# Keys, values and queries of two token tiles as one product of seven multiplications

## The chip, the cores and the metric

The kernel runs on one core of a Trainium2 chip. Its time is the device time of one execution in microseconds (us); of several executions the median counts, and less is better.

## The reference

A block of 2048 tokens with width 576: a layer norm, linear attention with 32 heads of width 18, and a feed-forward path of width 4608 whose gated result multiplies what attention gives. All inputs are float32. Cut to what matters:

```python
phi = lambda t: jnp.where(t > 0, t + 1, jnp.exp(t)) + 1e-6
xn = layernorm(x)                                   # x: (1, 2048, 576)
q, k, v = heads(xn @ wqkv)                          # wqkv: (576, 3 * 576), 32 heads of 18
pq, pk = phi(q), phi(k)
kv = jnp.einsum("bhsd,bhse->bhde", pk, v)           # one 18 x 18 state for each head
z = jnp.einsum("bhsd->bhd", pk)
num = jnp.einsum("bhqd,bhde->bhqe", pq, kv)
den = jnp.einsum("bhqd,bhd->bhq", pq, z)[..., None] + 1e-6
s = merge_heads(num / den) @ wo                     # wo: (576, 576)
g = silu(gelu(xn @ w1 + b1) @ w2 + b2)              # w1: (576, 4608), w2: (4608, 576)
return x + s * g
```

## The kernel before

**Number format.** A float32 value is split into a high part, rounded to the format that TensorE multiplies at full speed (fp32r), and a low part, the rest. A product of two such values is three matmuls: high by high, high by low, low by high. The 576 rows of a contraction are five k-tiles: four of 128 rows, and a fifth that holds 64 rows twice, high parts above low parts, so that it needs two matmuls and not three. A token tile is 128 tokens; there are NT = 16.

**Order.** The two attention stages stand under `in_order()`: on each engine the instructions run in the order in which the program text issues them. SyncE (SP) issues nearly all DMAs, in text order too. In the feed-forward the order is written out by a planner (`add`, `at_step`), which gives each step of a chunk its place beside the matmuls.

**Stage one, keys and values (loop `for t in range(NT)`, 0 to about 145 us).** For each token tile `load_x` brings the rows for `statistics` (two `bn_stats` on VectorE, the inverse root by `pow` on GpSimd, POOL). The first four tiles are normalized on ScalarE (L227) and transposed by TensorE. For the others x comes transposed from memory; `store_stats` writes mean and inverse deviation of the 128 tokens to memory, `load_stats` reads them back as a row on all partitions (`bc`), `center` subtracts on POOL (L282), `scale` multiplies on VectorE (L285), and `set_x_hi`, `set_x_lo` split. All parts stay on chip, as `xh` and `xl`. `project` (L310 to L325, its matmul is L321) multiplies the tile with the weights `wkv_h`, `wkv_l`: keys and a first group of values in 28 matmuls (tile `pk`), the other values in 14 (`pv`). `phi` makes three ScalarE passes (L334, L336, L338) and a VectorE maximum (L340). `state` (L379) adds the keys' products with the values, of the tile before, into the banks `ps_kva` and `ps_kvb`.

Beside this stand operands for the feed-forward. `w2_load` brings the blocks of W2 for one of nine chunks into a raw tile (`w2r`, two alternate), `w2_sum` (L405, POOL) forms two differences, `w2_hi` (L413, ScalarE) and `w2_lo` (L418, VectorE) split them, and `w2_store` writes them to memory; `we_*` do the same for sums of W1's last rows, in five parts.

**Between the stages.** `fold_wo` multiplies the masked state with the output weights and gives `kw`, which `split_kw` splits.

**Stage two, queries and output (loop `for i in range(1, NT + 4)`, about 162 to 283 us).** `query` multiplies a token tile with the query weights, 28 matmuls of `project` (tile `pq`); `phi` again; `by_sums` and `normalize` form the denominators (POOL, VectorE) and p = phi(q) / den on POOL (L753); `pad` (ScalarE) copies 64 columns; `transpose_p` transposes p on TensorE (tile `ptp`) and splits it; `attend` (matmul L788) multiplies it with `kw` in 28 matmuls, and the result goes to memory (`s_dram`):

```python
    for i in range(1, NT + 4):
        if 1 < i < NT:
            query(i)
        ...
        if 2 <= i < NT + 2:
            transpose_p(i - 2)
        if 2 <= i < NT + 1:
            pad(i - 1)
        beside(i, 2)
        if i < NT:
            normalize(i)
        if i >= 4:
            attend(i - 4)
```

Beside it `XSums` forms on VectorE the sums of x that the first feed-forward product needs, `Rest` gathers the 64 remaining rows through memory (L925 to L973), and W1 and W2 operands of the first chunks are loaded and split.

**The feed-forward.** Two halves of 1024 tokens, nine chunks each, 28 steps to a chunk of some 44.7 us. The first product (class `Up`, L1129 to L1185) takes a block 2 x 2 by 2 x 2 with seven block products in place of eight (sums of blocks as operands, the 64 rest rows added in), and so does the second (`product`, L1273). At the change of halves (640.9 to 685.6 us) the x operands of the second half are loaded by `load_x_part` (L1446) in seven transfers of 1 MB.

The functions that the change touches, as they stand before it:

## Time and profile before

| | before |
|---|---|
| median of three runs | 1103.26 us |
| lowest, highest | 1101.92, 1103.40 us |
| span of the profiled execution | 1096.2 us |
| TensorE matmuls (PE) | 1088.2 us busy, 99% |
| TensorE weight loads (PEld) | 1008.8 us, 92% |
| VectorE (DVE) | 829.5 us, 76% |
| ScalarE (ACT) | 491.3 us, 45% |
| GpSimd (POOL) | 471.5 us, 43% |
| mean granted TensorE clock | 0.999 |
| transfers | 262.54 MB, mean 239 GB/s |

The profile is of one execution. Its span is from the first to the last instruction; for its own time only the timed runs stand, whose median is 7.06 us above the span, so that a number of the profile is compared with 1096.2 and the kernel's time with 1103.26. A row of costly groups has line, engine, operation, result and operands, their shapes and the count, then the busy time of all and the mean ns of one, then the engine's idle time before them with the instruction that ended most of it. A row of the chain in order of time has start, length, engine, tile and line. A row of windows has the stretch, its length, and the busy time and the instructions of PE, PEld, DVE, ACT and POOL, then the granted clock, the share of the DMA engines and GB/s; where it begins with "a:b" the first figure after it is the length.

### The profile page before, as it was taken

To read this page: it belongs to the slowest core of one execution; us is meant where nothing else is said; L and a number is where in the kernel's file an instruction comes from. 1 tells how busy PE (TensorE), PEld (TensorE's weight loads), DVE (VectorE), ACT (ScalarE), POOL (GpSimd) and SP (SyncE) were. 2 spreads that over 40 slices of the span, in tenths; PEclk is the share of its full clock that TensorE was granted. 3 is DMA by queue.
4 is the path that set the end of the run, shared out by engine and by line. 5 is a ranking of instruction groups with operands and counts; after the bars stand their busy time and mean duration, and the time that the engine had idled before them with its cause. 6 is when DMAs were issued, how large, how long until landed. Compare 5 with 4: busy or idle time off the path is not lost.

```text
span 1096.2 us, 18083 instructions
## 1 busy us (share of the span) xinstructions
PE 1088.2 (99%) x6702; PEld 1008.8 (92%) x6702; DVE 829.5 (76%) x1132; ACT 491.3 (45%) x844; POOL 471.5 (43%) x403
## 2 busy tenths in 40 slices
PE   9999999999999999999999999999999999999998
PEld 8999989999898998989989989899898998989987
DVE  7787748888798888888888888667475584764856
ACT  6555555555545455454453544524234243242442
POOL 3676434323546446464554553424234143242340
PEclk9999999999999999999999999999999999999999
DMA  7898834675959558486585769978676676767452
GB/s 248 264 274 274 309 137 149 206 248 186 333 221 350 182 220 322 160 320 224 189 332 175 284 237 400 391 248 289 215 241 219 210 231 212 238 219 224 126 184 87
DMA packets 88400, 262.54 MB, mean 239 GB/s; under 512 B 11894, under 2 KB 24182, under 8 KB 85624
## 3 DMA queue, kind: packets, MB, share of 16 engines
q1 hardware_dynamic: 88312, 261.38, 69.3%
q8 instruction: 53, 0.87, 0.3%
q14 instruction: 35, 0.29, 0.1%
HBM read 164.24 MB, written 95.17 MB: 237 GB/s over the span
## 4 chain that ended last, share of the span: by engine, by line
PE 99%; DVE 1%; ACT 0%; issue 0%; POOL 0%; DVEq 0%; POOLq 0%
PE pm L1286 35%; PE a L1147 10%; PE e L1147 10%; PE zy L1147 10%; PE pk L321 6%; PE pq L321 5%; PE ps_s L788 5%; PE b L1147 5%; PE pv L321 4%; PE pd L1402 2%; PE ps_kva L382 1%; PE ptp L770 1%; PE ps_kw L707 1%; PE warm L369 0%; DVE wkv_l L364 0%; PE ps_kvb L382 0%
## 5 line engine op out<-in xcount | busy, mean ns | idle before, releaser
L1292 DVE TENSOR_TENSOR macc<-pm,macc 128x576 f32<-128x576 f32 x218 | 163.9, 752 | 49.9 <-PE pm L1286 48.4
L812 ACT CAST h_h<-g 128x512 fp32r<-128x512 f32 x204 | 121.9, 621 | 132.7 <-PE pm L1286 131.5
L815 DVE TENSOR_TENSOR h_l<-g,h_h 128x512 fp32r<-128x512 f32 x204 | 161.8, 800 | 0.0
L1252 POOL TENSOR_TENSOR mid<-g 128x512 f32<-128x512 f32 x34 | 43.9, 1292 | 108.1 <-ACT g L1155 108.1
L1246 POOL TENSOR_TENSOR g<-g 128x512 f32<-128x512 f32 x34 | 54.9, 1616 | 49.5 <-DVE h_l L815 28.4
L1155 ACT ACTIVATE g<-b,b1c 128x512 f32<-128x512 f32 x36 | 24.8, 690 | 102.5 <-DVE b L1173 102.5
L1164 ACT COPY mid<-a 128x512 f32<-128x512 f32 x36 | 21.1, 585 | 95.3 <-PE a L1147 95.3
L858 POOL TENSOR_TENSOR w1raw<-w1raw 128x256 f32<-128x256 f32 x18 | 13.3, 737 | 116.8 <-ACT h_h L812 68.2
L1167 DVE TENSOR_TENSOR mid<-b,mid 128x512 f32<-128x512 f32 x36 | 24.8, 690 | 45.0 <-PE b L1147 41.8
L1374 POOL TENSOR_TENSOR fin1l<-fin1h,fin1l 128x288 f32<-128x288 f32 x8 | 6.5, 811 | 118.4 <-DMA fin1l<-s_dram 69.6
L1249 POOL TENSOR_TENSOR g<-g 128x512 f32<-128x512 f32 x34 | 55.2, 1623 | 2.7
L1147 PE MATMUL a<-h0r,wa 128*128 128x512 f32 x144 | 50.4, 390 | 0.0
L1147 PE MATMUL a<-xh,wa 128*128 128x512 f32 x144 | 50.4, 390 | 0.0
L815 DVE TENSOR_TENSOR h_l<-mid,h_h 128x512 fp32r<-128x512 f32 x34 | 48.8, 1436 | 1.2
L1155 ACT ACTIVATE g<-e,b1c 128x512 f32<-128x512 f32 x36 | 24.8, 690 | 51.9 <-DVE e L1180 51.9
L753 POOL TENSOR_TENSOR pbuf<-phiq,den 128x576 f32<-128x576 f32 x16 | 19.4, 1213 | 63.6 <-DVE den L752 63.6
L1243 POOL TENSOR_TENSOR g<-g 128x512 f32<-128x512 f32 x34 | 44.1, 1296 | 2.7
L1180 DVE TENSOR_TENSOR e<-e,mid 128x512 f32<-128x512 f32 x36 | 24.8, 690 | 22.3 <-PE e L1147 22.3
L1170 DVE TENSOR_TENSOR mid<-zy,mid 128x512 f32<-128x512 f32 x36 | 24.9, 691 | 19.8 <-PE zy L1147 19.8
L1173 DVE TENSOR_TENSOR b<-e,mid 128x512 f32<-128x512 f32 x36 | 25.2, 700 | 18.5 <-PE e L1147 17.4
L321 PE MATMUL pk<-wkv_h,xh 128*128 128x288 f32 (+1 forms) x160 | 38.2, 321 | 0.4 <-ACT xh L248 0.4
L321 PE MATMUL pk<-wkv_l,xh 128*128 128x288 f32 (+1 forms) x160 | 38.4, 321 | 0.0
(857 smaller groups left out, 3646.5 us busy)
## 6 DMA issues: line engine op xcount, KB each, us to landing
we<-we_dram SPq DMA_DIRECT2D x36, 448.0 KB
w2raw<-w SPq DMA_DIRECT2D x10, 1152.0 KB
op<-w2o SPq DMA_DIRECT2D x18, 576.0 KB
w1raw<-w SPq DMA_DIRECT2D x18, 512.0 KB
op_a<-wa SPq DMA_DIRECT2D x18, 512.0 KB
op_c<-wc SPq DMA_DIRECT2D x18, 512.0 KB
op_d<-wd SPq DMA_DIRECT2D x18, 512.0 KB
wc<-op_c SPq DMA_DIRECT2D x18, 512.0 KB
```

Source lines behind the costliest of these rows:

```text
L321: nc.tensor.matmul(ps[:, h, : ws.stop - ws.start], st, w[:, k, ws], start=(begin and i == 0), stop=(end and i == len(seq) - 1), skip_group ...
L788: nc.tensor.matmul(ps[:, h, :HD], st[:, k, :], w[:, k, h * HD : (h + 1) * HD], start=(i == 0), stop=(i == len(seq) - 1),)
L812: nc.scalar.copy(pair[0], src)
L815: eng.tensor_tensor(pair[1], src, pair[0].bitcast(F32), op=SUB)
L1147: nc.tensor.matmul(ps, st, mv, start=first and n == 0, stop=n == len(seq) - 1, skip_group_check=True,)
L1155: nc.scalar.activation(g, ps, AF.Gelu_apprx_tanh, bias=b1c[:, f : f + 1])
L1243: tt(src[5, pr], A(1, 0), A(1, 1), op=ADD)
L1246: tt(src[6, pr], src[5, pr], A(0, 0), op=SUB)
L1249: tt(src[3, pr], A(0, 1), src[6, pr], op=SUB)
L1252: tt(src[7, pr], A(0, 0), A(1, 0), op=SUB)
L1286: nc.tensor.matmul(ps[:, q, :HD], hs[p][st][:, cs], m[:, p, :], start=(n == 0 and i not in CHAIN), stop=(n == 5), skip_group_check=True,)
L1292: nc.vector.tensor_tensor(dst, src, dst, op=ADD)
```

## The change

The token tiles go in eight pairs. For a pair, the normalized x of its two tiles by the columns of keys, values and queries (half of keys and values, a quarter of the queries: 432 columns in each of two banks) is one block product with seven multiplications (`product_x`), in the order `ORDER_X`. Each is 12 matmuls, with four more for the rest rows in products 2, 5, 3 and 4; `evict` adds the results up on VectorE through two tiles `u1`, `u2`. The eviction of product 3 and the last phi of a pair come at the start of the next (`pend`). The first pair is multiplied plainly, four times 28 matmuls (`plain_x`). Pairs 6 and 7 make keys and values alone, and their query columns after the loop (`pair(…, "q")`).

The operands of a pair (`OPS`: 14 blocks of 128 columns, high and low, with the sums of `x_sums`) are those of the first feed-forward product; they go to memory (`store_ops`) and come back in quarters before each half (`load_x_part`, 28 blocks a quarter tile, pieces of 512 bytes). x, which stays on chip before the change, and `XSums` and the weights of `project` go. Queries go to memory and come back for stage two (`store_q`, `load_q`).

The raw tile for the operands of W2 and W1's rows is one and not two. A `whole_round` is differences, high part, low part and stores of one part, then the load of the next. Rounds stand one in each of pairs 2 to 5, two in pairs 6 and 7, and the other six in the first iterations of `attend`. For token tiles the order of `attend` is 12, 13, 0 to 11, 14, 15; a half is now the pairs 0 to 3 or 4 to 7, so the feed-forward takes its tokens by `token_tile`. Its matmuls are the same in number and shape. The staging pool has four tiles and not six.

Cut to its core (in the full text the functions of the old stages go, with their loops):

```diff
-    def project(t, hi, lo, ps, order=PARTS, cols=(slice(0, HD), slice(HD, D)),
...
-    def w2_load(c):
-        t = w2p.tile([P, 3, 2, HD], F32, tag="w2r", name=f"w2r{c}")
-        nc.sync.dma_start(t.rearrange("p b a d -> p (b a d)"), w2[c][:, D:])
-        w2raw[c] = t
...
-    def query(t):
-        pq[t] = bank2(f"pq{t}")
-        project(t, wq_h, wq_l, pq[t])
...
-            project(t, wkv_h, wkv_l, pk, order, cols=(slice(0, HD), slice(HD, D + VB)))
...
-            query(i)
...
+NPR = NT // 2
+KV = HD
+QC = D // 4
+NW = KV + QC
...
+    def token_tile(half, t):
+        b, q = divmod(t, QH)
+        return NPR * half + 2 * q + b
...
+    W_OF = {1: "B11", 2: "B21", 3: "B22", 4: "T4", 5: "T1", 6: "T2", 7: "T3"}
+    X_OF = {1: 10, 2: 12, 3: 8, 4: 0, 5: 6, 6: 4, 7: 2}
+    XLO = 14
+    REST_T1, REST_T0, REST_D = range(3)
+    REST_OF = {2: (REST_T0, 0), 5: (REST_T1, 1), 3: (REST_D, 1), 4: (REST_T1, 0)}
+    ORDER_X = (1, 2, 6, 7, 5, 4, 3)
...
+    def x_sums(p, rest=True):
+        r, tt = R[p], nc.vector.tensor_tensor
+        tt(r[:, 9:11], r[:, 0:2], r[:, 3:5], op=ADD)
+        tt(r[:, 7:9], r[:, 9:11], r[:, 13:15], op=SUB)
+        tt(r[:, 5:7], r[:, 13:15], r[:, 0:2], op=SUB)
+        tt(r[:, 11:13], r[:, 15:17], r[:, 7:9], op=SUB)
...
+    def store_ops(p):
+        nc.sync.dma_start(x_dram[p // QH, p % QH], OPS[p].bitcast(F32))
...
+    def product_x(p, i, ps, part, first):
+        (wh, wl), a, o = W[W_OF[i]], X_OF[i], OPS[p]
+        seq = []
+        for k in range(2):
+            seq += [(o[:, a + k], wh[:, k]), (o[:, a + k], wl[:, k]), (o[:, XLO + a + k], wh[:, k])]
+        if i in REST_OF:
+            r, n = REST_OF[i]
+            seq += [(XR[p][:, r], t[:, n]) for t in W["R"]]
+        for n, (st, mv) in enumerate(seq):
+            mm(ps, st, mv, part, first and n == 0, n == len(seq) - 1)
...
+        def load(self):
+            t = tw.tile([P, 3, 2, HD], F32, tag="raw", name=f"w2r{self.c}", bufs=1)
+            nc.sync.dma_start(t.rearrange("p b a d -> p (b a d)"), w2[self.c][:, D:])
...
+        def sums(self):
+            nc.gpsimd.tensor_tensor(self.src[5][0], self.src[5][1], self.src[5][0], op=SUB)
+            nc.gpsimd.tensor_tensor(self.src[6][0], self.src[6][0], self.src[6][1], op=SUB)
...
+    def whole_round():
+        if loaded:
+            round_sums(), round_hi(), round_lo(), round_store()
...
+    def evict(p, i, ps, part):
...
+        elif i == 7:
+            nc.vector.tensor_tensor(
+                u_part(u2, part), ps_part(ps, part), u_part(u1, part), op=ADD
+            )
...
+        for i in ORDER_X:
+            if i in (1, 6, 7):
+                bank[{1: 0, 6: 1, 7: 2}[i]] = bank2(f"x{part}{p}{i}")
+            b = {1: 0, 2: 0, 6: 1, 5: 1, 3: 1, 7: 2, 4: 2}[i]
+            product_x(p, i, bank[b], part, i not in (2, 3))
+            if i == 2:
+                if part != "q":
+                    phi_hi(f"k{p}0", kv_of(bank[0]))
+                if part != "kv":
+                    copy_q(T0, 0, bank[0], part)
+            elif i == 3:
+                pend.append(lambda ps=bank[1]: evict(p, 3, ps, part))
+            else:
+                evict(p, i, bank[b], part)
+            hooks.get(i, lambda: None)()
+
...
+    ROUND_OF = {2: 1, 3: 1, 4: 1, 5: 1, 6: 2, 7: 2}
...
+        def operands():
+            scale(prep)
+            store_rest(prep)
+            x_sums(prep)
+            op_tiles(prep)
...
+        def after1():
+            if prep and not first:
+                operands()
+            if first:
+                for k in range(2):
+                    w_hi("T1", k), w_lo("T1", k, dve)
+                center(2)
+            if qp:
+                phi_q_hi(qp[0])
+            if prep and not first:
+                operands_hi()
+            if first:
+                for k in range(2):
+                    w_hi("T4", k), w_lo("T4", k, pool)
+            state(p - 1)
+            if not first:
+                next_statistics()
...
+        def after7():
+            phi_max(f"k{p}0", k_bufs[0], kv_of(banks[p][0]))
+            if qp:
+                phi_q_max(qp[0]), store_q(qp[0])
+                phi_q_hi(qp[1]), phi_q_max(qp[1]), store_q(qp[1])
+            if first:
+                operands()
+                operands_hi()
+            elif nxt:
+                center(nxt)
...
+        def after5():
+            if first:
+                rest_lo(prep), x_lo_ops(prep, 10, 14), x_lo_ops(prep, 0, 10)
+                store_ops(prep)
+                next_statistics()
+                center(nxt)
+                round_load()
+            for _ in range(ROUND_OF.get(p, 0)):
+                whole_round()
...
+            phi_k1_max(p - 1)
+            pend.pop()()
...
+    pair(NPR - 2, "q", {})
+    pend.pop()()
...
+    pair(NPR - 1, "q", {6: make_zb, 7: after7, 5: after5, 4: after4, 3: after3})
...
+    X_SEGS = {
+        "h0": ((10, 4, 0),), "l0": ((24, 4, 0),), "h1": ((0, 4, 0),), "l1": ((14, 4, 0),),
+        "s2": ((4, 2, 0), (18, 2, 2)), "s1": ((6, 2, 0), (20, 2, 2)), "s4": ((8, 2, 0), (22, 2, 2)),
+    }
...
+    def load_x_part(half, k, t):
+        for a, n, to in X_SEGS[k]:
+            for c in range(QH):
+                nc.sync.dma_start(
+                    t[:, to : to + n, c * P : (c + 1) * P].bitcast(F32),
+                    x_dram[half, c, :, a : a + n],
+                )
...
+    for j in range(NT):
+        attend(j)
+        if j + 6 < NT:
+            load_q(j + 6)
+        if j + 2 < NT:
+            transpose_p(j + 2)
+        if j + 3 < NT:
+            pad(j + 3)
+        if j + 4 < NT:
+            by_sums(j + 4)
+            denominators(j + 4)
+            p_mult(j + 4)
+        beside(j)
+        if j < 9 and loaded:
+            whole_round()
```

More of the change, by code (lines that the diff above doesn't have):

```diff
@@ L34 @@
 NG = len(GROUPS)
-NSTG = 6
+NSTG = 4
 QH = 4
@@ L760, in pad, with folds, after7, after5 @@
-    def pad(t):
-        pb = p_bufs[t % 2]
-        nc.scalar.copy(pb[:, D:], pb[:, 512:D])
+        krs.append(kr4)
+        yield
+    groups = fold_wo()
+    def folds(n):
+        for _ in range(n):
+            next(groups)
+    def after7():
+        folds(1)
+    def after5():
+        folds(2)
+        by_sums(0), by_sums(1)
+    def after4():
+        folds(1)
+        denominators(0), p_mult(0)
+    def after3():
+        folds(1)
+        denominators(1)
+    pair(NPR - 1, "q", {6: make_zb, 7: after7, 5: after5, 4: after4, 3: after3})
```

1357 lines of the change are left out of this document (713 added, 644 removed), and 4 rows, old and new, of the table SUMS.

## The prediction

> **What bounds the kernel now.** I read first the page, its shares and its chain.
>
> ```profile
> span 1096.2 us, 18083 instructions
> PE 99%; DVE 1%; ACT 0%; issue 0%; POOL 0%; DVEq 0%; POOLq 0%
> ```
>
> TensorE is the chain from one end to the other, so the change is worth what it takes from TensorE, less every wait that it opens there. Next the chain in order of time, for the two attention stages:
>
> ```profile
> 32.55 2.92 PE pv L321 x14
> 35.47 4.49 PE pk L321 x28
> 41.02 2.93 PE pv L321 x14
> ...
> 179.09 3.73 PE pq L321 x28
> 183.37 3.73 PE ps_s L788 x28
> ```
>
> A token tile costs 8.47 us in the first stage (32.55 to 41.02: 2.92 + 4.49 of products, 1.06 of `state`) and in the second 3.73 for queries, 0.55 for transposes (182.82 to 183.37) and 3.73 for `attend`: 16.5 us in all. Last the windows, for what lies beside it:
>
> ```profile
> 49.50:145.30 95.80, 95.80 (x588) 92.90 (x587) 74.19 (x90) 52.30 (x102) 60.87 (x55) 1.00 0.89 284
> 162.20:283.20 121.00, 121.00 (x922) 120.76 (x921) 99.79 (x143) 65.56 (x110) 45.78 (x36) 1.00 0.61 201
> ```
>
> TensorE never stops in either stage, while VectorE is busy 77 and 82% and the transfers 89 and 61%. The cover is wide but not idle, and the change shortens it.
>
> **What the change takes from TensorE.** Today's 70 matmuls a tile cost 2.92 + 4.49 + 3.73 = 11.13 us, 178.1 for 16 tiles. After it a pair takes seven products of 12 matmuls and four rests of 4: 100 matmuls of 432 columns. That width isn't in the trace; it lies between these:
>
> ```profile
> 1087.33 0.68 PE L1402 MATMUL pd<-w__11094,hp 128*128 128x384 f32 x3
> 1087.85 0.68 PE L1402 MATMUL pd<-w__11114,hp 128*128 128x384 f32 x3
> ```
>
> Three of 384 start 0.52 us apart, 0.173 each; one of 288 takes 3.73/28 = 0.133, one of 450 2.92/14 = 0.209. On the line through the first two, 432 takes 0.193 (0.20 if 450's row is nearer). The plain first pair is 112 x 0.193 = 21.6 us, pairs 1 to 5 19.3 each, pairs 6 and 7 (their query columns apart, at 288) 150 x 0.133 = 20.0 each: 158 us. **Term: -20 us** (-16 by the other price). Transposes, `state`, `fold_wo`, `attend` and the feed-forward matmuls stay in number.
>
> **What it adds beside TensorE, and which waits come of it.** Prices:
>
> ```profile
> L285 DVE TENSOR_TENSOR xt<-xt,bc 128x640 f32<-128x640 f32 x12 | 11.1, 922 | 0.5 <-POOL xt L282 0.5
> L196 DVE BATCH_NORM_STATS2 st<-x 128x6 f32<-128x288 f32 x16 | 7.2, 450 | 3.0 <-DMA x<-x 3.0
> L340 DVE SCALAR_TENSOR_TENSOR phik<-pk,ek 128x576 f32<-128x576 f32 x16 | 12.0, 752 | 8.8 <-ACT ek L338 8.6
> L418 DVE TENSOR_TENSOR w2o<-w2r,w2o 128x576 fp32r<-128x576 f32 x18 | 19.1, 1098 | 0.2
> L364 DVE TENSOR_TENSOR kw_l<-kr,kw_h 128x576 fp32r<-128x576 f32 x3 | 3.5, 1180 | 0.2 <-ACT kw_h L363 0.2
> L405 POOL TENSOR_TENSOR w2r<-w2r 128x576 f32<-128x576 f32 x18 | 28.8, 1598 | 15.6 <-DVE phik L340 8.5 <-DMA w2r<-w 6.4
> L282 POOL TENSOR_TENSOR xt<-xt,bc 128x640 f32<-128x640 f32 x12 | 20.2, 1684 | 11.5 <-DMA bc<-st_dram 6.5 <-ACT vb L375 2.2 <-ACT ek L334 2.0
> L201 POOL TENSOR_TENSOR mv<-mv,nhalf 128x1 f32<-128x1 f32 x16 | 13.6, 848 | 27.2 <-DVE mv L200 25.8 <-ACT xn L227 0.8 <-ACT xh L244 0.6
> L334 ACT ACTIVATE ek<-pk 128x576 f32<-128x576 f32 x16 | 10.4, 649 | 8.6 <-PE pk L321 8.6
> L336 ACT ACTIVATE ek<-ek 128x576 f32<-128x576 f32 x16 | 11.1, 695 | 0.0
> L338 ACT ACTIVATE ek<-ek,tiny 128x576 f32<-128x576 f32 x16 | 12.4, 778 | 0.5
> L413 ACT CAST w2o<-w2r 128x576 fp32r<-128x576 f32 x18 | 11.5, 672 | 2.5 <-POOL w2r L405 2.5
> ...
> w2r<-w SPq DMA_DIRECT2D x9, 864.0 KB
> op<-w2o SPq DMA_DIRECT2D x18, 576.0 KB
> ...
> 183.28 0.33 SPq L945 DMA_DIRECT2D rr_dram<-wa_rest0q  x1
> ...
> 185.29 0.32 SPq L950 DMA_DIRECT2D wa_rest0ef<-rr_dram  x1
> ...
> 676.00:680.00 4.00, 4.00 (x32) 4.00 (x31) 3.44 (x6) 1.52 (x4) 0.00 (x0) 1.00 1.00 418
> 36.00:42.00 6.00, 6.00 (x41) 5.91 (x40) 4.53 (x9) 2.31 (x5) 5.82 (x5) 1.00 0.91 221
> ```
>
> Phi is 2.1 us of ScalarE (the three ACTIVATE rows). What follows are waits of TensorE, so none of them can fall below nothing. A store and the load that waits for it start 2.0 us apart for 256 KB; at full rate (418 GB/s) the bytes are 0.6 of that, so landing costs 1.4 beyond them.
>
> *Rounds beside `attend`.* The operands that `w2_load` to `w2_store` make today in stage one are made in rounds through one raw buffer, where today two alternate: a round's load is issued only behind the stores of the round before. Five W2 rounds stand in `attend`'s first six iterations, in program order on every engine. One costs two POOL subtractions 3.2, the last ScalarE copy 0.7, VectorE's low part 1.1, three issues 1.0, then the second store and the load, 1.47 MB at 418 GB/s, 3.5, and landing 1.4: 10.9 us. Behind the copy on ScalarE's queue stand the evictions of `attend` and of the next transposes; TensorE runs two tiles ahead and then waits for them. A tile is 4.28 us of TensorE: 5 x (10.9 - 4.28) = **+33 us** (20, if the slack of two tiles is saved once and the loads come early, to 45 with mean transfers at 243 GB/s, 221/0.91).
>
> *Two rounds in one pair* (pairs 6 and 7). From the end of product 5: its eviction 0.9, the first round's low part 1.1, issues 1.0, store and load 1.8 MB 4.3, landing 1.4, subtractions 3.2, copy 0.7, low part 1.1. Only then comes product 4's eviction on VectorE 0.8, phi 2.1, its maximum 0.75, product 3's eviction 0.9, and `state` of that pair may start: 18.2 us. TensorE has products 4 and 3 (4.3) and the next pair's first (1.6) to do: a wait of 12.3, twice: **+23 us** (14 to 28).
>
> *Pairs 1 to 5.* A ring of waits goes through the statistics of the pair after next: scaling 1.85, five operand sums 1.7 (1152 columns by L285), four statistics 1.8, `pow` 0.85, store and reload of the row 2.0 + 2.5, centering 3.4, the round's subtractions 3.2, copy and low part 1.8, eviction of product 4, phi, maximum, eviction of product 3 (0.75 + 2.1 + 0.75 + 1.3): 24 us, 24.7 with the small operations, against 19.3 + 2.1 of TensorE. 3.2 for each of pairs 2 to 5, and some 7 for pair 1, whose operands stand ahead of its product 5's eviction: **+20 us** (2 to 32; nothing, had the row landed a pair earlier).
>
> *Start.*
>
> ```profile
> 8.01 0.76 PE L321 MATMUL pk<-wkv_h,xh 128*128 128x288 f32 x4 [0.40 <-ACT xh L248]
> 14.26 1.20 ACT L227 ACTIVATE xn<-x,mv 128x576 f32<-128x576 f32 x2
> ```
>
> The first product ends at 8.0 + 28 x 0.193 = 13.4. The next token tile is normalized at 14.3 to 15.5, which tile 0's values cover today; then come its transposes, two weight splits and the operand's copy, until about 18: 4 us. Before the fourth plain product ScalarE still has phi and four copies: 3 more, and 1 before tile 3's transposes. **+8** (4 to 11).
>
> *Fold.* Today queries run on through `fold_wo`'s results. Now, between the last product and the first `attend`, ScalarE does two phi of queries (4.3), copies and five splits, VectorE five low parts at up to 1.18; TensorE has 2 us of transposes and folds for it. **+9** (6 to 14).
>
> *Transfers before the feed-forward.* Behind the last round stand operands of the first half, 7.3 MB in pieces of 512 bytes that SP issues one quarter tile at a time (today they stay on chip or are made there), rest rows, weights, queries and s: about 15.5 MB, 37 us at 418 GB/s, 64 at 243; TensorE has eight `attend`s, 33 us. **+10** (0 to 31), near the fast end since most bytes are in long pieces. At the change of halves forty transfers of short pieces take the place of seven: 17.6 us or 30 for 7.3 MB; nothing waits there today: **+2** (0 to 12).
>
> Sum: -20 + 33 + 23 + 20 + 8 + 9 + 10 + 2 = +85 us on a span of 1096.2. The median of the runs shown, 1103.26, lies 7 above the span, and I add to it: **1188 us**.
>
> **The rivals.**
>
> *TensorE alone decides.* Every wait is hidden and the time is 1103.3 - 20 = 1083, faster. For it: the 99% chain, and VectorE's 74 of 95.8 us. It decides if a round takes under 4.3 us, which the 1.47 MB, 3.5, and landing, 1.4, alone exceed. Chance 0.06. That the change doesn't do what it says is no case of its own: the program has the 432-column matmuls.
>
> *Only the rounds wait.* The ring of pairs 1 to 5, start, fold and operand loads fit: -20 + 33 + 23 = +36: 1139. For it: before keeps TensorE full at 89% transfers. Against: the ring is priced by busy times alone. Chance 0.20.
>
> *Transfers bound the rest.* Short pieces move at 243 GB/s and both loads take their upper ends: +21 + 10 more: 1219. Chance 0.15.
>
> *The clock falls in the waits.*
>
> ```profile
> 1090.39 0.50 PE L1402 MATMUL pd<-w__11150,hp 128*128 128x192 f32 x3
> ...
> 1092.00:1094.00 2.00, 0.00 (x0) 0.00 (x0) 0.99 (x3) 0.00 (x0) 0.00 (x0) 0.84 0.67 257
> 1094.00:1096.20 2.20, 0.00 (x0) 0.00 (x0) 0.00 (x0) 0.00 (x0) 0.00 (x0) 0.50 0.12 38
> ```
>
> TensorE ends at 1090.9 and the granted clock goes to 0.5 at about 1093.4 (0.84 is two thirds of 2 us at 1.0): a wait over 2.5 us is followed by matmuls at half clock. No row shows the return; if it takes as long as the fall, a wait costs 1.25 more. Some ten are that long (start, five pairs, two doubles, fold, feed-forward; in the rounds it is hidden): +13: 1201. The Trainium skill (TensorE: Matmul & The Clock Gate, the part on the clock gate) has the clock halved after an idle window of about 3.4 us and back after as long a stretch of work. The trace agrees on the half and has it sooner; by the page's figure my estimate is 10 x 1.7 = 17 us, 1205. Chance 0.12, beside the 0.46 of the forecast.
>
> **How the numbers follow.** Forecast 1188, 0.46; only the rounds 1139, 0.20; transfers 1219, 0.15; clock 1201, 0.12; faster 1083, 0.06; no change 0.01. The range is 1133 to 1230: it takes in the rounds alone with a few us below, and above the transfers with half the spread of the unknown prices; outside are the fast case and the tails. Faster by over 0.2% (about what a measurement here can tell) 0.06, within it 0.01, slower 0.93.
>
> **What would show it.** Right: idle time of ScalarE's copy `w2o` behind POOL, of POOL behind the load `w2r`, and of TensorE's `ptp` behind ScalarE's `pad`, about 7 us each, in five iterations of `attend`; two waits of some 12 us at `ps_kva` after pairs 6 and 7, shorter ones after the others; matmuls of 432 columns at 0.193 us. Wrong: a chain that is TensorE at 99% again, or `attend` at 4.3 us a tile while rounds run.

## The result, and the profile after

The changed kernel takes 1270.7 us (four runs, 1267.1 to 1273.2) where the kernel before takes 1102.64 in the same series: ratio 1.1529, 95% interval 1.1501 to 1.1556. It is slower by 168 us. The direction was forecast, 1188 was not, and the range ended at 1230. Later series ran on chips on which the kernel before took 1097.7 to 1098.6 us; for comparison every ratio below is also given times 1102.64.

From the page after: the span, the busy time, and the chain by engine and by line.

```profile
span 1265.4 us, 17904 instructions
...
PE 1129.8 (89%) x6480; PEld 1034.5 (82%) x6480; DVE 856.0 (68%) x1221; ACT 502.8 (40%) x835; POOL 481.9 (38%) x410
...
PE 65%; DMA 6%; SPq 3%; DVE 3%; ACT 2%; POOL 1%; issue 1%; POOLq 0%; DVEq 0%; ACTq 0%
PE pm L1517 29%; PE zy L1378 9%; PE e L1378 9%; PE a L1378 9%; PE b L1378 5%; PE pd L1637 2%; DMA w2r<-w 1%; SPq L1273 1%; PE xq L344 1%; DMA q<-q_dram 1%; PE ps_s L1066 1%; DMA rq_dram<-wa_rest0s 1%; DMA rxm<-rq_dram 1%; DMA we<-we_dram 0%
```

TensorE was the chain at 99%; now it is 65%, and 63% are the feed-forward (L1517, L1378, L1637). The shares add up to 81%, since the chain could be followed back only to 245.7 us. Between 245.7 us and the feed-forward, TensorE holds little of it; transfers, SP's queue, VectorE and ScalarE hold most. What happened ahead of 245.7 has to be read from the windows and waits below. No engine has much more to do than before (VectorE 829.5 to 856.0; TensorE is busy for 1129.8 us and not 1088.2 although its work fell, since matmuls behind a wait run slower): the time is in waits. Where they stand, by windows of the changed kernel (PE, PEld, DVE, ACT and POOL busy, granted clock, share of the DMA engines, GB/s), cut at the marks of the program: the plain pair; pairs 1 to 5; pairs 6 and 7 with the query columns of 6; query columns of 7 and the fold; the first eight iterations of `attend`; the last eight; the feed-forward.

```profile
8.08:45.07 36.99, 30.47 (x128) 27.36 (x128) 25.77 (x35) 19.69 (x37) 17.74 (x15) 0.82 0.30 115
45.07:195.35 150.28, 126.12 (x602) 116.87 (x600) 103.61 (x191) 70.84 (x103) 43.43 (x39) 0.86 0.58 200
195.35:270.89 75.54, 47.30 (x311) 46.30 (x310) 31.05 (x50) 25.31 (x37) 14.17 (x29) 0.80 0.44 157
270.89:303.56 32.67, 18.79 (x92) 14.72 (x90) 15.89 (x32) 14.99 (x31) 9.01 (x7) 0.77 0.19 60
303.56:381.69 78.13, 49.74 (x264) 45.25 (x265) 40.90 (x55) 20.52 (x39) 37.64 (x28) 0.76 0.70 233
381.69:442.53 60.84, 41.81 (x260) 40.13 (x260) 22.11 (x43) 13.87 (x27) 19.66 (x16) 0.81 0.97 309
442.53:1265.40 822.87, 810.59 (x4806) 739.35 (x4806) 613.02 (x811) 334.34 (x560) 338.59 (x268) 0.99 0.70 240
```

A matmul of 432 columns starts 0.197 us after the one before (the row of four takes 0.95 and is followed 0.79 later), one of 288 columns 0.133:

```profile
69.64 0.95 PE L344 MATMUL xall<-wT3h,OPS 128*128 128x432 f32 x4
70.43 0.56 PE L344 MATMUL xall<-wT3l,OPS 128*128 128x432 f32 x2
```

With these, 1.05 a tile for `state` and the prices of before for the rest, TensorE's own work in each window can be taken off; what is left is loss. The feed-forward is counted from the matmul of its first tile on that takes the rest rows, at 442.53 here and at 284.42 before; its loss is against the 811.8 us that followed there.

| window | length | work | loss | forecast |
|---|---|---|---|---|
| plain pair | 37.0 | 24.6 | 12.4 | 8 |
| pairs 1 to 5 | 150.3 | 109.0 | 41.3 | 20 |
| pairs 6, 7, queries of 6 | 75.5 | 39.6 | 35.9 | 23 |
| queries of 7, fold | 32.7 | 16.0 | 16.7 | 9 |
| `attend`, first eight | 78.1 | 34.2 | 43.9 | 33 |
| `attend`, last eight | 60.8 | 34.5 | 26.3 | 10 |
| feed-forward | 822.9 | 811.8 | 11.1 | 2 |

The losses are 187.6 us where 105 were forecast. TensorE's work up to there, 266.0 with the 8.1 of the beginning, is 18.4 less than the 284.4 of before; -18.4 + 187.6 = 169.2, the difference of the spans. So one term of the sum was right, TensorE's, and every one of the seven losses was too small.

The waits of TensorE up to 480 us, and after that (engine, tile and line waiting, and for what; total, number, longest):

```profile
PE ptp L1011 <- ACT s L1071: 22.4, 5, 6.5
PE ps_kva L418 <- DVE kph L378: 21.2, 6, 12.4
PE xq L344 <- ACT u L731: 15.9, 2, 11.3
PE ptp L1011 <- POOL vb L922: 12.1, 5, 6.4
PE a L1378 <- DMA rxm<-rq_dram: 7.9, 1, 7.9
PE ps_s L1066 <- ACT kw_h L1054: 7.0, 1, 7.0
PE xall L344 <- DVE u L734: 6.8, 1, 6.8
...
PE ps_kva L418 <- ACT vb L400: 4.4, 1, 4.4
```

```profile
PE a L1378 <- DMA we<-we_dram: 7.0, 1, 7.0
```

The forecast's two long waits after pairs 6 and 7 are there at their size: 12.4 at `ps_kva` and 11.3 at the query columns of pair 6, for 12.3 each. The five of `attend`'s rounds are there too, though shorter as idle time (22.4 in all) than as loss. Idle time is not all of it: TensorE is busy for longer than its work, 126.1 for 109.0 in pairs 1 to 5, because its matmuls run at half clock behind the longer waits (granted clock 0.86). Whether that is a cost of its own was the first thing to find out.

### The profile page after: what moved, and what is told of

Its sections match the earlier page's. It is cut to its first block, busy times and chain, and to the rows that moved or that the text cites. A ratio compares the mean times of both kernels' runs of the same rounds, so it can differ in the third digit from the quotient of the medians.

```text
span 1265.4 us, 17904 instructions
## 1 busy us (share of the span) xinstructions
PE 1129.8 (89%) x6480; PEld 1034.5 (82%) x6480; DVE 856.0 (68%) x1221; ACT 502.8 (40%) x835; POOL 481.9 (38%) x410
## 4 chain that ended last, share of the span: by engine, by line
PE 65%; DMA 6%; SPq 3%; DVE 3%; ACT 2%; POOL 1%; issue 1%; POOLq 0%; DVEq 0%; ACTq 0%
PE pm L1517 29%; PE zy L1378 9%; PE e L1378 9%; PE a L1378 9%; PE b L1378 5%; PE pd L1637 2%; DMA w2r<-w 1%; SPq L1273 1%; PE xq L344 1%; DMA q<-q_dram 1%; PE ps_s L1066 1%; DMA rq_dram<-wa_rest0s 1%; DMA rxm<-rq_dram 1%; DMA we<-we_dram 0%; PE ps_kw L958 0%
## 5 line engine op out<-in xcount | busy, mean ns | idle before, releaser
L1483 POOL TENSOR_TENSOR mid<-g 128x512 f32<-128x512 f32 x34 | 43.9, 1291 | 120.2 <-ACT g L1386 120.2
L1386 ACT ACTIVATE g<-b,b1c 128x512 f32<-128x512 f32 x36 | 24.9, 690 | 105.3 <-DVE b L1404 105.3
L463 DVE TENSOR_TENSOR w2o<-w2r,w2o 128x576 fp32r<-128x576 f32 x18 | 24.1, 1337 | 53.7 <-ACT w2o L459 52.6
L1066 PE MATMUL ps_s<-kw_h,th 128*128 128x288 f32 x160 | 42.6, 354 | 13.4 <-ACT kw_h L1054 7.0
L1378 PE MATMUL a<-h0r,wa 128*128 128x512 f32 x144 | 50.4, 390 | 0.0
L1378 PE MATMUL a<-h0f,wa 128*128 128x512 f32 x144 | 50.4, 390 | 0.0
L418 PE MATMUL ps_kva<-kph,vb 128*127 128x126 f32 x128 | 26.1, 368 | 25.6 <-DVE kph L378 21.2
L1011 PE MATMUL ptp<-ident,vb 128*128 128x128 f32 x80 | 15.8, 338 | 34.5 <-ACT s L1071 22.4
L418 PEld LDWEIGHTS ps_kva<-kph,vb 128*127 128x127 f32 x128 | 23.2, 271 | 27.8 <-DVE kph L378 23.2
L1066 PEld LDWEIGHTS ps_s<-kw_h,th 128*128 128x128 f32 x160 | 31.8, 234 | 16.1 <-ACT kw_h L1054 7.4
```

What stands on the lines that cost most here:

```text
L418: nc.tensor.matmul(dst, v_bufs[j][:, i, : G + 1], k_bufs[j][:, g : g + n], start=(p == 0 and j == 1 and i in (0, 4)), stop=(p == NPR - 1 a ...
L1066: nc.tensor.matmul(ps[:, h, :HD], st[:, k, :], w[:, k, h * HD : (h + 1) * HD], start=(i == 0), stop=(i == len(seq) - 1),)
L1378: nc.tensor.matmul(ps, st, mv, start=first and n == 0, stop=n == len(seq) - 1, skip_group_check=True,)
L1386: nc.scalar.activation(g, ps, AF.Gelu_apprx_tanh, bias=b1c[:, f : f + 1])
L1483: tt(src[7, pr], A(0, 0), A(1, 0), op=SUB)
```

## The experiments

**Is the half clock a cost?** `fill` adds matmuls that nobody needs ahead of the waits:

```diff
+    def fill(n):
+        w = W["B11"][0][:, 0]
+        for _ in range(n):
+            nc.tensor.matmul(
+                ps_kv[1][:, 128:], w[:, :P], w[:, :384], start=False, stop=False,
+                skip_group_check=True,
+            )
...
+            fill(FILL.get((p, 1), 0))
             state(p - 1)
...
+        if 3 <= j < 8:
+            for _ in range(30):
+                nc.tensor.matmul(
+                    filler[:, :384], kw_h[:, 0, :P], kw_h[:, 0, :384], start=True, stop=True
+                )
```

> 168 filler matmuls of 384 columns (0.173 us each, into columns of a PSUM bank that nobody reads) stand before the waits of pairs 2, 4, 6, 7 and of both groups of query columns, and 30 before the transposes in each of five iterations of attend; nothing else differs. Theory, the clock is a part of the loss of its own: after a wait the matmuls of 432 columns run at 0.36 us in place of 0.197 for 3 to 6 us, and where TensorE is late next this is paid. Then pairs 2 to 7 and the query columns lose 10 to 16 us less, while attend gains nothing, since its period of 12.1 us is set by the load of the raw tile and not by TensorE: 1254 to 1261. Rival, half clock is hidden everywhere, since the next wait takes it up: 1267 to 1273. Rival, it is paid everywhere: some 11 us less in attend too, 1240 to 1248.

Ratio 1.1525 (1.1475 to 1.1575), 1270.8: no change. Windows of pairs 2 to 7 and of the iterations 3 to 7 of `attend`, of the changed kernel and then of `fill`:

```profile
85.26:248.97 163.71, 133.48 (x722) 126.06 (x721) 99.13 (x178) 70.77 (x101) 43.98 (x59) 0.87 0.56 192
321.34:381.69 60.35, 33.81 (x165) 30.73 (x166) 29.75 (x39) 14.68 (x28) 29.98 (x20) 0.74 0.78 260
```

```profile
83.50:247.20 163.70, 145.36 (x822) 137.66 (x821) 100.53 (x183) 70.71 (x101) 43.95 (x59) 0.96 0.58 195
319.54:381.72 62.18, 52.87 (x315) 49.85 (x315) 29.87 (x39) 14.76 (x29) 30.33 (x20) 0.95 0.76 253
```

A hundred more matmuls in the pairs, the mean clock at 0.96 and not 0.87, and the six pairs take 163.70 us for 163.71. My theory of a clock cost of 10 to 16 us falls; the rival, that the next wait takes it up, holds. It says more: some 55 us of filler (318 matmuls at 0.173 us) don't move the end, so that in these stretches the loss is the chain of the other engines and transfers. The plain pair, pair 1, the fold and the end of `attend` got little filler or none; for them the question stays open.

**The rounds.** `no_rounds` cuts all fourteen to their stores; it leaves out the operands that the rounds make.

```diff
     def whole_round():
-        if loaded:
-            round_sums(), round_hi(), round_lo(), round_store()
+        if rounds:
+            r = rounds.pop(0)
+            if isinstance(r, W2Round):
+                v = blank[0][:, : 4 * HD].rearrange("p (a b c) -> p a b c", a=2, b=2)
+                r.op = {5: v, 6: v}
+            else:
+                r.t = blank[0].rearrange("p (v b c) -> p v b c", v=2, b=WB)
+            r.store()
```

> The fourteen rounds keep their stores (of a tile of zeros) and leave out loads, differences and splits, so the operands that they make are zeros. Theory, the rounds are the largest part: 39 us in attend's iterations, 24 at the two waits after pairs 6 and 7 with some 5 of half clock behind them, and about 5 in pairs 2 to 5, where a round's parts stand ahead of an eviction: 1270 - 73 = 1197 (1185 to 1210), with attend at 4.3 us a tile as long as the rounds lasted. Rival, the transfers set the end of attend anyway, and what the rounds gave up comes back as a longer wait for the operands of the feed-forward: 1220 to 1235.

Ratio 1.0945 (1.091 to 1.0979), 1206.8: 64 us less. Its windows of pairs 6 and 7, and of the first and last eight iterations:

```profile
187.40:219.80 32.40, 31.19 (x241) 30.95 (x240) 17.54 (x32) 15.01 (x22) 0.00 (x0) 1.00 0.65 247
261.00:303.10 42.10, 38.34 (x265) 37.02 (x265) 26.25 (x45) 13.73 (x28) 19.42 (x14) 0.91 0.74 254
303.10:377.00 73.90, 45.29 (x263) 43.36 (x262) 22.29 (x41) 13.93 (x28) 20.25 (x17) 0.75 0.95 304
```

Pairs 6 and 7 take 32.4 us for 53.6, the first eight iterations 42.1 for 78.1. But the last eight take 73.9 for 60.8: 13 us come back there, with the DMA engines 95% busy. Both theories had a part: the rounds are the largest cost, and the end of `attend` has a bound of its own.

**What bounds a round.** `raw2` gives the rounds in `attend` a second raw tile.

```diff
+    def raw_at(c):
+        return (more[0], "raw2") if more and c % 2 == 0 else (tw, "raw")
...
-            t = tw.tile([P, 3, 2, HD], F32, tag="raw", name=f"w2r{self.c}", bufs=1)
+            pool, tag = raw_at(self.c)
+            t = pool.tile([P, 3, 2, HD], F32, tag=tag, name=f"w2r{self.c}", bufs=1)
```

> In attend the rounds alternate between two raw tiles, so that the load of the next W2 block runs while this one is split; the pairs are as they were. Theory, the ring goes through the raw tile (splits 3.2 + 2, store issues 2, load 6.2): with the load ahead the period is that of subtractions, splits and stores, 7 to 8 us and not 12.1, in five iterations: 1270 - 22 = 1248 (1243 to 1256). Rival, the transfers set the period (2.6 MB an iteration at 300 GB/s, 8.8 us): 1254 at best, and the end of attend waits for operands as long as before. Rival, the stores are the ring through the two operand tiles: no change, 1265 to 1272.

Ratio 1.1425 (1.1385 to 1.1466), 1259.8: 11.4 us less. In the changed kernel the loads of the raw tile stand 12.4 and 11.9 us apart (left out is all else that SP issues):

```profile
333.31 0.37 SPq L447 DMA_DIRECT2D w2r<-w  x1
...
345.67 0.38 SPq L447 DMA_DIRECT2D w2r<-w  x1
...
357.60 0.37 SPq L447 DMA_DIRECT2D w2r<-w  x1
```

In `raw2` they stand 9.4 and 10.2 us apart (330.60, 339.98, 350.14), and the first eight iterations take 63.9 us for 78.1, at 280 GB/s and 83% busy DMA engines. I had 7 to 8 us a round, and 1243 to 1256 in all. The rival of the transfers gave 8.8, but it is not what these rounds wait for. GpSimd's waits from 300 to 375 us, in the changed kernel and in `raw2`:

```profile
POOL vb L922 <- DVE den L918: 29.4, 7, 6.7
POOL w2r L452 <- DMA w2r<-w: 12.2, 4, 3.6
```

```profile
POOL vb L926 <- DVE den L922: 34.3, 9, 6.9
```

The wait for the load of the raw tile is gone. What is left is a ring of instructions in text order: GpSimd's two differences start at 353.68; ScalarE's copy, VectorE's low part, the split of p and the denominators follow, then GpSimd's product `vb`, and the next differences start at 362.79. That is 9.1 us without a transfer in it; in one of the four rounds, where VectorE formed sums of the rest rows beside them, the two differences took 3.7 us and not 2.9 and the ring 10.1. Of the 14 us that the rounds gained, the end of `attend` took 5 back.

**The operands' way back.** `long_x` lays the operands of a half out as they are read:

```diff
-    x_dram = dram.tile([2, QH, P, 28, P], F32, name="x_dram")
+    x_dram = dram.tile([2, P, 28, QH * P], F32, name="x_dram")
...
-            for c in range(QH):
-                nc.sync.dma_start(
-                    t[:, to : to + n, c * P : (c + 1) * P].bitcast(F32),
-                    x_dram[half, c, :, a : a + n],
-                )
+            nc.sync.dma_start(t[:, to : to + n].bitcast(F32), x_dram[half, :, a : a + n])
```

> The operands of a half lie in memory as the feed-forward reads them: the store of a pair writes pieces of 512 bytes, and a load takes whole parts in pieces of 4 to 8 KB, ten transfers for a half in place of forty. Theory, the last eight iterations of attend (60.8 us for 32.6 of TensorE's work) and the change of halves (10 us) wait for SP's issues and for short pieces: 15 to 25 us less in the one, 7 to 10 in the other, and up to 5 more in the pairs for the stores in short pieces: 1240 to 1250. Rival, the bytes set the end whatever their pieces: 1262 to 1270. Rival, the stores in short pieces hold up the rows of the statistics, which stand behind them on the queue: slower, up to 1285.

Ratio 1.139 (1.1352 to 1.1429), 1255.9: 15.3 us less, where I expected 20 to 30. The feed-forward takes 813.3 us (1253.2 less 439.9) and waits for nothing: all but 1.5 of the 11.1 lost there were the forty transfers in short pieces (their number and their pieces changed together; which of the two it was is not separated). The last eight iterations take 50.9 us, and the row says why not less:

```profile
389.10:440.00 50.90, 41.63 (x262) 40.35 (x261) 23.23 (x43) 13.87 (x27) 19.47 (x16) 0.86 0.99 367
```

The DMA engines are 99% busy at 367 GB/s: bytes bound it. The pairs, whose stores now go in short pieces, take 5.5 us longer (query columns of pair 6 from 254.5 on, for 249.0).

**The start.** `dve_sums` moves four weight differences from GpSimd to VectorE, `row_first` puts the statistics' row ahead of the operand store, `late_phi` moves two phi behind the splits of kw.

```diff
-    for k in range(2):
-        w_sum("T2", k, pool), w_sum("T4", k, pool)
     x_sums(0, rest=False)
+    for k in range(2):
+        w_sum("T2", k, dve), w_sum("T4", k, dve)
```

> In the start, four weight differences (L310, 2.3 us each on GpSimd) go to VectorE, behind the operand sums of the first pair. In the changed kernel those sums (L249 to L252, 256 columns each) take 2.15 to 2.28 us while GpSimd works on the differences and 0.42 later. Theory, two engines that read and write SBUF hold each other up: the sums take 0.42, the differences some 1.0 each on VectorE, and the operands of pair 1 are ready about 3 us earlier, the end of pair 1 comes 3 to 6 us earlier: 1262 to 1267 at 1270 for the changed kernel. Rival, the sums are long for another reason (their operands come late): they stay at 2.2 and the start gets 4 us longer. Rival, the gain is taken up by the wait of pair 2 for the row of the statistics: pair 1 ends earlier, and the total is the same within 2 us.

```diff
-                store_ops(prep)
                 next_statistics()
+                store_ops(prep)
                 center(nxt)
```

(and the same for the first pair)

> In pairs 0 and 1 the statistics of the pair after next, with their store and reload as a row, are issued ahead of the 1.8 MB store of operands, behind which they stand in the changed kernel (store issued at 85.4, row there at 97.0: 11.6 us where the prediction took 4.5). Theory, that queueing is what makes pair 2 long (35.5 us, with 6.8 at its fifth product): the row is there 5 to 6 us earlier, pair 2 takes 28 to 30 us, and the total falls by 5 to 8. Rival, a small store and its reload take 10 us by themselves: pair 2 stays at 35. Rival, pair 2 gets shorter and pair 4, which waits for the ring next, takes it back: less than 2 us.

```diff
-    for t in TO[-2:]:
-        phi_q_hi(t), phi_q_max(t), store_q(t)
     transpose_p(1)
...
     for k in range(KT):
         split_kw(k, dve)
+    for t in TO[-2:]:
+        phi_q_hi(t), phi_q_max(t), store_q(t)
```

> The phi of the last two query tiles (six ScalarE passes, 4.3 us, needed only at the end of attend) moves from ahead of the weight splits of attend to behind them. Theory, ScalarE's order is what the first attend waits for (7.0 us behind the high parts of kw): it starts 4 to 5 us earlier, and attend's rounds, which start from the load of the raw tile, gain the same only if that load was also late; the first waits of attend's rounds grow by what is not: total less by 1 to 5 us. Rival, the splits on VectorE (0.9 us late) or the fold's own chain take its place at once: no change.

Ratios 1.1518 (1.1494 to 1.1541), 1.1518 (1.1494 to 1.1542) and 1.1514 (1.1489 to 1.1538): by the time, none can be told from the changed kernel's 1.1529. By the profiles each did what it says in its place. The groups of the operand sums on VectorE, in the changed kernel beside GpSimd's differences, and in `dve_sums` without them:

```profile
L251 DVE TENSOR_TENSOR R<-R 128x256 f32<-128x256 f32 x1 | 2.3, 2277 | 0.0
```

```profile
L251 DVE TENSOR_TENSOR R<-R 128x256 f32<-128x256 f32 x1 | 0.4, 418 | 0.0
```

Five times shorter, and pair 1 takes 36.6 us and not 40.2. The row of the statistics, by SP's and POOL's timelines, in the changed kernel (operand store, two stores of statistics, two loads of the row; then the centering) and in `row_first`:

```profile
83.67 0.35 SPq L275 DMA_DIRECT2D x_dram<-OPS  x1
85.42 1.63 SPq L216 DMA_DIRECT2D st_dram<-mv  x2
91.30 0.80 SPq L221 DMA_DIRECT2D bc<-st_dram  x2
```

```profile
97.04 3.13 POOL L239 TENSOR_TENSOR R<-R,bc 128x640 f32<-128x640 f32 x2 [10.48 <-DMA we<-w1e]
```

```profile
85.18 1.49 SPq L216 DMA_DIRECT2D st_dram<-mv  x2
88.00 2.83 SPq L221 DMA_DIRECT2D bc<-st_dram  x2
90.92 0.38 SPq L275 DMA_DIRECT2D x_dram<-OPS  x1
```

```profile
92.42 3.15 POOL L239 TENSOR_TENSOR R<-R,bc 128x640 f32<-128x640 f32 x2 [6.11 <-DMA bc<-st_dram]
```

The load of `we`, which the row of the changed kernel names, is no operand of the centering; `bc` is. From the stores of the statistics to the centering 7.2 us and not 11.6; pair 2 takes 30.0 us and not 35.5 (pair 1 takes 42.2 and not 40.2). In `late_phi` the part from the query columns of pair 7 to the first `attend` takes 29.2 us and not 32.7. How much of that reaches the feed-forward differs. `attend` starts 2.7, 4.3 and 5.2 us earlier in the three profiles; the matmul with the rest rows, at 442.53 in the changed kernel, stands at 442.53, 440.38 and 437.94. With `dve_sums` the stretch of transfers before the feed-forward waits all of the gain away (the rival, in another place than I had put it), with `row_first` half, with `late_phi` little. Each is one execution, and the times don't tell them apart.

**Together.** `all5` holds `raw2`, `long_x`, `dve_sums`, `row_first` and `late_phi`.

> Five edits in one: the second raw tile in attend, operands in long pieces, the weight differences on VectorE, the row ahead of the operand store, the late phi. Theory, each takes away a wait in a place of its own, and TensorE was late at each: the gains add, 13 + 15 + 4 + 6 + 3 = 41 us, to about 1229 (1222 to 1236) at 1270 for the changed kernel, which is still 11 to 12% above the kernel before: what is left are the waits of the two rounds after pairs 6 and 7, the splits of the rounds in attend and the end of attend. Rival, the transfers before the feed-forward are the bound of the whole stretch: the gains of the start are waited away there, and the sum stays at the two edits that touch transfers, 1240 to 1246.

Ratio 1.1181 (1.1157 to 1.1205), 1232.9: 38 us less, where the five alone give 11.4 + 15.3 + 1.2 + 1.2 + 1.7 = 31. By the times these two can't be told apart. In the profiles the matmul with the rest rows comes 27.0 us earlier (415.56), where the five alone come 8.9, 2.6, 0.0, 2.2 and 4.6 earlier, 18.3 in all: with the transfers relieved, more of what the start gains seems to get through. Three more kernels stand on it: `early_x` loads the operands earlier in `attend`, `one_round` leaves one round in each of pairs 6 and 7, `all7` does both.

```diff
-    FIRST_AT = {5: "h0", 6: "l0", 7: "s2", 8: "h1", 9: "l1", 10: "s1", 11: "s4"}
+    FIRST_AT = {0: "l0", 1: "l1", 2: "s1", 3: "s4", 5: "h0", 6: "s2", 7: "h1"}
```

> The kernel with the five edits, and in it four of the seven parts of the first half's operands are loaded from the first iterations of attend on (0 to 3) and the other three, which need rest rows, at 5 to 7, where they stood at 5 to 11. The bytes are the same. Theory, the end of attend is bound by bytes (54.5 us at 359 GB/s, the DMA engines 97% busy) while they were 83% busy in its first 63 us: spread, the two stretches together need 37.3 MB, some 98 us at 380 GB/s and not 118, of which the rounds, whose loads are held up, take part back: 6 to 15 us less than the five edits, 1214 to 1223 at 1229 for them. Rival, the rounds' own loads wait behind the operands, and what the end gains the rounds lose: 1226 to 1232. Rival, the order of SP's queue and not the bytes is the bound of the end: 1226 to 1232 too, but with the DMA engines below 90% busy there.

Ratio 1.1124 (1.1091 to 1.1156), 1226.6: 6.3 less, at the low end of what I expected. Windows of the two halves of `attend` in `all5`, and in `early_x`:

```profile
298.30:361.50 63.20, 44.84 (x264) 40.82 (x264) 41.88 (x54) 24.64 (x46) 38.20 (x28) 0.87 0.84 281
361.50:415.50 54.00, 40.60 (x260) 39.02 (x260) 24.30 (x43) 13.73 (x27) 19.70 (x16) 0.85 0.97 358
```

```profile
296.30:362.80 66.50, 47.71 (x264) 43.69 (x264) 36.75 (x54) 24.64 (x46) 37.69 (x28) 0.83 0.89 327
362.80:409.90 47.10, 39.71 (x261) 38.83 (x262) 24.04 (x43) 13.74 (x27) 20.27 (x16) 0.86 0.97 336
```

The end is 6.9 us shorter, the rounds 3.3 longer, and the DMA engines are 89 and 97% busy: the same bytes, spread. Together that is 113.6 us for 117.2, where I had some 98: the rounds lose half of what the end gains, as the rival said. The other 2.0 us lie ahead of `attend`, which the edit does not touch.

```diff
-    ROUND_OF = {2: 1, 3: 1, 4: 1, 5: 1, 6: 2, 7: 2}
+    ROUND_OF = {2: 1, 3: 1, 4: 1, 5: 1, 6: 1, 7: 1}
```

(with the raw tiles of the eight rounds in `attend` still alternating)

> The kernel with the five edits, and pairs 6 and 7 hold one round each; the two left stand in attend, which then holds eight. Theory, the second round in a pair costs a wait of 11 to 13 us, as the prediction had it (end of the first round's store and load of the next raw tile ahead of the last phi), and in attend with two raw tiles a round costs 9.3 less 4.3, 5 us: 24 + some 5 of half clock less, 10 more, and the end of attend as long as before or a little shorter, since its transfers start later but its iterations are fewer: 1212 to 1222 at 1229. Rival, the wait of pairs 6 and 7 is set by the round that stays: 1228 to 1238.

Ratio 1.1019 (1.0986 to 1.1053), 1215.0: 17.9 less, a little more than expected. Its waits of TensorE from pair 6 to the query columns of 7 are 6.2 us, where `all5` has 30.7:

```profile
PE ps_kva L419 <- DVE kph L379: 4.1, 2, 3.4
PE xkv L345 <- DVE vb L397: 1.6, 1, 1.6
PE xq L345 <- ACT u L736: 0.5, 1, 0.5
```

```profile
PE ps_kva L419 <- DVE kph L379: 16.7, 2, 14.9
PE xq L345 <- ACT u L736: 11.2, 1, 11.2
PE xkv L345 <- DVE vb L397: 1.6, 1, 1.6
PE xkv L345 <- DVE u L739: 1.2, 1, 1.2
```

> The five edits, the early operands and one round a pair together. Theory, the waits are of different places and add: 1229 - 10 - 12 = 1207 (1198 to 1215), 9 to 10% above the kernel before, since two things stay that no order of this program takes away: TensorE's work of a pair stands within evictions of 0.75 to 1.05 us on VectorE and the ring through the statistics, and the rounds and operands are moved while TensorE has 4.3 us a tile to do. Rival, with eight rounds in attend the early operands hold up more loads, and both gains together are no more than the larger: 1215 to 1222.

Ratio 1.0932 (1.09 to 1.0965), 1205.4: 27.5 less than `all5`; the two gains (6.3 and 17.9) add, within the intervals. It is the fastest form of the change that computes all, and 9.3% slower than the kernel before. Last, `all5_no_rounds`: the five edits but for the second raw tile, which has no use then, and `no_rounds`; it too leaves out the operands of the rounds.

> The kernel with the five edits (the second raw tile is not needed then), the fourteen rounds cut to their stores of zeros: the operands that they make are left out. Theory, this is the floor of the change without its rounds: pairs 6, 7 and the query columns 42 us and not 76.6, attend's first eight iterations 42 and not 63, the end of attend 55 to 62: 1182 (1174 to 1192), so that even with rounds that cost nothing the kernel is 6 to 8% slower than before, by the pairs, the fold and the operands' way through memory. Rival, the rounds are all that keeps it from the kernel before: below 1130.

Ratio 1.0664 (1.0628 to 1.07), 1175.9: with rounds that cost only their stores the kernel is still slower. Its pairs 3 to 5 take 23.1 us each (113.0 to 182.3), 1.3 over TensorE's 21.8, so that the ring hardly waits there once the rounds are out of it; pairs 1 and 2 still take 38.7 and 30.1.

## Why the prediction was wrong

**TensorE, -20:** -18.4. The price of 432 columns, 0.193 by the line between two rows, was 0.197.

**The rounds beside `attend`, +33:** 43.9 in the first eight iterations. The mechanism, the ring through one raw tile, was right: `raw2` and `no_rounds` take 14 and 36 us off that stretch. The size was off: a round takes 11.9 to 12.4 us and not 10.9, and five of them give some 40 of the 43.9. The term that was mis-sized is the transfer: 4.9 us for the second store, the load and landing at the full rate, where the load alone takes 6.1 from its issue to the first difference (345.67 to 351.78). VectorE's low part took 1.8 for 1.1; what else stands in the ring took 0.9 less. With the load taken out, a ring of 9.1 to 10.1 us through GpSimd, ScalarE and VectorE is close behind, which the working did not price.

**Two rounds in one pair, +23:** twice 12.3 is 24.6, so that the term is 1.6 below its own working. The two waits came at 12.4 and 11.3, and `one_round` takes them away (17.9 us off `all5`, with the two rounds that it puts into `attend` paid). The rest of the 35.9 are a wait of 3.4 at the `state` in pair 6, one of 1.1 behind it, and 7.7 us by which TensorE is busy for longer than its work (47.3 for 39.6), at a granted clock of 0.80; by `fill` this is no cost of its own.

**Pairs 1 to 5, +20:** 41.3. The step that failed is the one ring of 24.7 us for all five. Pairs 3 to 5 are as it says in their mean, 24.9; one by one they take 23.4, 27.7 and 23.5, so that the agreement is partly luck. Pairs 1 and 2 are not in a steady ring: they take 40.2 and 35.5, 32 us over their work, where I had 7 and 3. For pair 2 the term that was mis-sized is "store and reload of the row 2.0 + 2.5": 11.6 us, as the two stores of 1 KB stood behind one of 1.8 MB. `row_first` gives 4.4 of it back, and pair 2 gets 5.5 shorter. For pair 1 it is the operand sums at 0.42 that took 2.2 beside GpSimd (3.6 us of the pair). The rest of pair 1, some 15 us, no run takes away. By the rows its waits are 10.9 us (the longest, 4.4, for ScalarE's copies of values, which stand in its queue behind splits for pair 1), and for 7.5 us TensorE is busy for longer than its work (29.3 for 21.8) at a granted clock of 0.75. Its cause stays open.

**Start, +8, and fold, +9:** 12.4 and 16.7. In the start the waits are 6.5 us, in the places that were named; the other 5.9 are matmuls at a granted clock of 0.82 (30.5 busy for 24.6), which the term left out, and whether they cost anything was not tried. In the fold the waits are 13.9: 7.0 for the high parts of `kw`, 4.6 for ScalarE's `u` at the query columns of pair 7, 2.3 for p. ScalarE's order was named and is 3.5 us by `late_phi`; the rest stays open.

**Transfers before the feed-forward, +10, of 0 to 31, "near the fast end since most bytes are in long pieces":** 26.3, near the slow end. This is a step that failed, by 16 us, and a part of what the start gains is lost there too. The working had 15.5 MB, of which by its own count nearly half, 7.3, goes in pieces of 512 bytes; at 309 GB/s over 60.8 us the stretch moved 18.8. It also had the full rate of 418 GB/s, which none of the stretches of 40 us and more shown here reached: 309 with the short pieces, 367 with long ones at 99% busy. 18.8 MB at 367 are 51 us, which is what `long_x` took.

**Change of halves, +2, of 0 to 12:** 11.1, nearly all of it the forty transfers in short pieces, by `long_x`.

**The rivals.** "Transfers bound the rest" (1219, 0.15) named the failing step with the right ends: 26 and 11 where it had 31 and 12. It too had the other terms at their forecast, so that 1219 is nearer for one reason only. "The clock falls in the waits" (+13) is refuted as a cost in pairs 2 to 7 and in `attend`'s rounds, though the clock fell as it said. The Trainium skill (TensorE: Matmul & The Clock Gate, HAM oscillation) shows a kernel in which the half clock after a wait for transfers costs a part of the time; here, where another chain sets the next wait, `fill` shows no cost: 163.70 us for 163.71 in the six pairs.

So no single term explains the miss. Four of the seven losses (pairs 1 to 5, the two rounds, start, fold) lie above the upper end of their own ranges. What the rows share is that each term was priced alone, as if its transfers did not stand behind those of another part, and one engine's instructions behind those of the next pair; this is shown for the row of pair 2 and the operand sums of pair 1, and argued for the rest.

## What to carry to other kernels

Taking work off the engine that is the chain pays only while its cover lasts: here 18.4 us of matmuls went, and the preparing that had hidden beside them opened 188 us of loss. Price a transfer that others wait for by what is queued ahead of it and by the rate of the whole stretch, not by its own bytes at full rate: 11.6 for 4.5 us, 18.8 MB at 309 to 367 for 15.5 at 418. And before counting a slow clock as a loss, give that engine more to do in its waits: if the end doesn't move, the loss is elsewhere.

## What the runs showed of the hardware

**The clock's return.** In the changed kernel TensorE's last matmuls before a wait start at 101.1 and end at 101.7; the granted clock is 0.67 in the half microsecond from 104.0 and 0.50 from 104.5. Work comes back at 108.5, and the clock is 0.50 until 114.0, 0.59 in the next half microsecond and 1.00 from 114.5, after 6 us of matmuls at 0.36 us:

```profile
101.13 0.56 PE L344 MATMUL xall<-wT3h,OPS 128*128 128x432 f32 x2
108.50 1.09 PE L344 MATMUL xall<-wT1h,OPS 128*128 128x432 f32 x2 [6.81 <-DVE u L734]
...
114.42 0.56 PE L344 MATMUL xall<-wT4h,OPS 128*128 128x432 f32 x2
```

I had taken the return to be as long as the fall, 2.5 us. It has no fixed length: in the same trace work that begins at 80.61 has its clock back in the half microsecond from 83.5 (0.81), after some 3 us, and work that begins at 60.47 in that from 66.5 (0.87), after some 6. The Trainium skill (TensorE: Matmul & The Clock Gate, The HAM clock gate) gives both some 3.4 us in a window that runs freely; the fall is sooner here, and the return lies on both sides of it.

**VectorE beside GpSimd.** Sums of two SBUF operands at 0.42 us took 2.15 to 2.28 while GpSimd ran differences of 2.33 us each. The Trainium skill (SBUF — State Buffer, two separate sides) says that such instructions of the two engines lock a shared pair of ports for a whole instruction; the rows agree, since each sum took about as long as one difference of GpSimd.

**A small store behind a large one.** The two stores of 1 KB, issued 1.75 us after one of 1.8 MB, let the load that waits for them go 5.9 us after their issue, and 2.8 us when the large one stood behind. The Trainium skill (DMA: Bandwidth & Descriptors, queues, rings and completion order) has the signal of a transfer land only after every earlier write of the same DMA engine, which agrees. The figures would also fit small stores whose own bytes came after those of the large one; no run here tells the two apart.
